# A Fourier and mixture-of-experts kernel: one sum of each fold moved into a DMA, and side work spread over the steps

## Chip, cores, metric

The kernel runs on one core of a Trainium2 chip. The metric is the device time of one execution in microseconds (us). The profile is one execution taken by the hardware profiler; its engines are PE (TensorE, with its weight loads as PEld), DVE (VectorE), ACT (ScalarE), POOL (GpSimd) and SP (the queue that issues most DMAs).

## The reference, cut to what matters

```python
X = np.fft.fft(np.fft.fft(x, axis=1), axis=2).real   # x: 8 x 3072 x 256, fp32
x = X.reshape(24576, 256)
g = x @ w_gate                                        # 256 x 1536
x = (g * sigmoid(g) * (x @ w_val)) @ w_out            # back to 256 columns
logits = x @ moe2_w_gate                              # 8 experts
# experts take tokens in falling order of logits, each up to 3072 of them
# out[mask] = relu(x[mask] @ w1[e]) @ w2[e]
```

## The kernel before, in words

Phase 1 computes the two-dimensional transform, the gated layer and the routing logits; phase 2 routes and runs the experts. The change is in phase 1.

Phase 1 goes through 48 tiles of 512 tokens, six for each of the eight batches. A tile has NF = 12 steps, one for each block of 128 hidden columns, and g counts the steps of all tiles (576). Step g in the main loop (lines 674 to 702) issues this: on PE the products Q (line 381) into the one Q bank; on ACT the copy qs of Q (681); on PE the products Pp; on ACT hi(g-2) (687), on POOL lo(g-2) (688); on DVE `columns(g)`, which is two T operations that read Q (392) and two G operations (393, 394); on ACT the silu sl(g-1) (695); on DVE the product hh(g-1) of sl and G, both in SBUF (400); on PE the twelve matmuls of `out_proj(g-3)` into Y (412). When a tile's last out_proj is through (its step 2 of the following tile) `finish` copies Y on ACT and moves the logits on POOL (420 to 426). Every engine takes what is issued to it in this order.

Side work is a set of Python generators. `advance(s)` runs each of them up to its next `yield`; half step A(g) = 2g is at the front of step g, Z(g) = 2g + 1 at its end. What stands in Z(g) is therefore queued behind step g's work on each engine, and what stands in A(g + 1) right behind that and ahead of step g + 1's. The side work:

- Transform halves (`fft_half`, lines 339 to 368; registered in lines 630 to 645). During tile t - 1 the x of tile t is computed, in a sine and a cosine half. A half has its matmuls into the one F bank (`fft_mm`, 300 to 326), then the copy od on ACT (351), a subtraction and an addition into ab on DVE (355 or 359, and 360), for the sine half also a one-row multiply by -1 (362); then xh on ACT (366) and xl on POOL (367). Before, the sine half starts at Z(1) and the cosine half at Z(4) of the tile.
- Folds (`fold`, 116 to 137; registered 646 to 661). Each batch from the second on has six x tiles of 512 KB, loaded by SP (113). POOL adds halves into fa (120), then makes fb (124, 127) and z (131, 134); these sums feed the transform. One operation every step, five steps a fold, from step 14 of the batch before on. `fold_special` does a last row at the end (142 to 152). xs has two buffers.
- The choice (`choose`, 775 to 795; registered 666 to 672): for each 16 columns of logits five DVE pieces, one per half step, from step 6 of every fourth tile on.
- A mini tile (437 to 495) runs in tiles 42 to 44.

```python
for g in range(total + LAG):
    advance(2 * g)
    ...
    advance(2 * g + 1)
```

Of the kernel before, what the change touches and what calls it, by code (L numbers as in the profile page):

```python
# [9 lines left out]
F32 = mybir.dt.float32  # L10
# [5 lines left out]
ALU = mybir.AluOpType  # L16
AX = mybir.AxisListType

P = 128
B = 8  # L20
S = 3072
D = 256
N = B * S
F = 1536
NF = F // P
# [61 lines left out]
def phase1(ctx, tc, io, yscr, Lall, ident, idt, NT, choice=None):  # L87
    nc = tc.nc
# [3 lines left out]
    work = ctx.enter_context(tc.tile_pool(name="work", bufs=2))  # L92
# [18 lines left out]
    def load_x(b, i):  # L111
        xs = work.tile([P, 4, D], F32, tag="xs", bufs=2, name="xs")
        nc.sync.dma_start(xs.rearrange("p m d -> p (m d)"), io["x"][b, i])
        return xs

    def fold(b, i, xs, eng, tags=(("fa", 1), ("fb", 1))):

        (ta, na), (tb, nb) = tags
        a = work.tile([P, 2, D], F32, tag=ta, bufs=na, name="fa")
        eng.tensor_add(a, xs[:, 0:2, :], xs[:, 2:4, :])  # L120
        yield
        yield
        bb = work.tile([P, 2, D], F32, tag=tb, bufs=nb, name="fb")
        eng.tensor_add(bb[:, 0, :], a[:, 0, :], a[:, 1, :])
        yield
        yield
        eng.tensor_sub(bb[:, 1, :], a[:, 0, :], a[:, 1, :])
        yield
        yield
        z = work.tile([P, 2, 2, P], F32, tag=f"z{i}", bufs=2, name=f"z{i}")  # L130
        eng.tensor_add(z[:, 0], bb[:, :, 0:P], bb[:, :, P:D])
        yield
        yield
        eng.tensor_sub(z[:, 1], bb[:, :, 0:P], bb[:, :, P:D])
        zt[b, i] = z
        yield
        yield
# [198 lines left out]
        nc.sync.dma_start(tb, tscr[b : b + 1, (t % 6) * 256 : (t % 6 + 1) * 256].broadcast_to([P, 256]))  # L336
        return tb

    def fft_half(t, sine, tb, res, bk=("F", 1), eng=nc.gpsimd):

        b, h, q = t // 6, (t // 3) % 2, t % 3
        lead = 1 if (h == 0 and q == 0) else 0
        n = P + lead

        par = (1 - h) if sine else h
        z = [zt[b, i][:, int(sine), par, :] for i in range(6)]
        pp = bank(*bk)
        fft_mm(pp, z, e768s[b % 2] if (h == 0 and not sine) else None, h, q, sine)
        yield
        od = work.tile([P, 129], F32, tag="od", bufs=1, name="od")  # L350
        nc.scalar.copy(od[:, :n], pp[:, 256 : 256 + n])
        ab = work.tile([P, 256], F32, tag="ab", bufs=2, name="ab")
        first = ab[:, 0:P][:, ::-1]
        if not sine:
            nc.vector.tensor_sub(first, pp[:, lead:n], od[:, lead:n])
            if lead and "R" in mini:
                nc.vector.tensor_copy(mini["R"][:, b : b + 1], ab[:, P - 1 : P])
        else:
            nc.vector.tensor_sub(first, od[:, lead:n], pp[:, lead:n])
        nc.vector.tensor_add(ab[:, P - lead : 256], pp[:, 0:n], od[:, 0:n])  # L360
        if sine:
            nc.vector.tensor_scalar_mul(ab[0:1, :], tb[0:1, :], -1.0)
        yield
        hi = work.tile([P, 256], F32R, tag=f"x{int(sine)}h", bufs=2, name="xh")
        lo = work.tile([P, 256], F32R, tag=f"x{int(sine)}l", bufs=2, name="xl")
        nc.scalar.copy(hi, ab)
        eng.tensor_sub(lo, ab, hi.bitcast(F32))
        res[sine] = (hi, lo)
# [68 lines left out]
    def mini_tile():  # L437

        xs = {}
        r0 = work.tile([1, B], F32, tag="tz", bufs=1, name="t15r")  # L440
        nc.sync.dma_start(r0, t15scr.rearrange("b o -> o b"))
        for n in ("R", "T"):
            for a in range(2):
                xs[n, a] = work.tile([P, P], F32R, tag=f"m{n}{a}", bufs=1, name=f"m{n}{a}")
                nc.gpsimd.memset(xs[n, a].bitcast(F32), 0.0)
        hs = [[work.tile([P, 4, P], F32R, tag=f"z{2 * j + a}", bufs=2, name=f"hT{a}") for a in range(2)] for j in range(3)]
        for t in hs:
            for a in range(2):
                nc.gpsimd.memset(t[a].bitcast(F32), 0.0)
        yield  # L450
        yield
        for n, src, k in (("R", mini["R"], P), ("T", r0, 1)):
            nc.vector.tensor_copy(xs[n, 0][0:k, 0:B], src)
            nc.vector.tensor_sub(xs[n, 1][0:k, 0:B], src, xs[n, 0][0:k, 0:B].bitcast(F32))
        yield
        for j in range(3):
            sl = work.tile([P, 4, D], F32, tag="xs", bufs=2, name="xs").rearrange("p a b -> p (a b)")
            for gv in range(2):
                pp = bank("F", 1)
                n = 0  # L460
                for cs, k in ((0, "R"), (1, "T")):
                    for a, d in order:
                        nc.tensor.matmul(pp, xs[k, d], Wb[j][:, cs, gv, a, :], start=(n == 0), stop=(n == 5))
                        n += 1
                yield
                if gv == 0:
                    nc.scalar.activation(sl[0:B, 0:512], pp[0:B, :], AF.Silu)
                else:
                    nc.vector.tensor_mul(sl[0:B, 512:1024], pp[0:B, :], sl[0:B, 0:512])
                yield  # L470
            pt = bank("F", 1)
            for i in range(4):
                nc.tensor.transpose(pt[:, i * P : i * P + B], sl[0:B, 512 + i * P : 512 + i * P + P], ident[0:B, 0:B])
            yield
            pv = pt.rearrange("p (i k) -> p i k", i=4)[:, :, 0:B]
            nc.scalar.copy(hs[j][0][:, :, 0:B], pv)
            nc.vector.tensor_sub(hs[j][1][:, :, 0:B], pv, hs[j][0][:, :, 0:B].bitcast(F32))
            yield
        for _ in range(4):
            yield  # L480
        pp = bank("F", 1)
        for c in range(NF):
            for i, (a, d) in enumerate(((0, 0), (0, 1), (1, 0))):
                nc.tensor.matmul(pp[:, 0:EXT], hs[c // 4][a][:, c % 4, :], Wo[c // 2][:, c % 2, d, :], start=(c == 0 and i == 0), stop=(c == NF - 1 and i == 2))
            if c % 4 == 3 and c < NF - 1:
                yield
                yield
        yield
        ys = work.tile([B, EXT], F32, tag="ys", bufs=1, name="ysm")
        nc.vector.tensor_copy(ys, pp[0:B, 0:EXT])  # L490
        lm = work.tile([B, E], F32, tag="lm", bufs=1, name="lm")
        nc.vector.tensor_copy(lm, ys[:, D:EXT])
        nc.vector.tensor_copy(ys[:, D : D + 1].bitcast(I32), idt[0:B, NCOL : NCOL + 1])
        nc.sync.dma_start(yscr[3 * P - 1 : N : S, :], ys)
        nc.sync.dma_start(Lall[P - 1 : P, 2 : 4 * NT : 24, :], lm)

    def off_peak(gen, s):

        s0 = s
        while True:  # L500
            if (s == s0 or s % (2 * NF) > NF or s % (2 * NF) == 0) and next(gen, gen) is gen:
                return
            s += 1
            yield
# [4 lines left out]
    def at(s, gen):  # L509

        side.setdefault(s, []).insert(0, gen)
# [113 lines left out]
    A, Z = lambda g: 2 * g, lambda g: 2 * g + 1  # L625
# [4 lines left out]
    for t in range(1, NT):  # L630
        res = {}
        g0 = (t - 1) * NF + (7 if t == 1 else 0)

        def start(t=t, res=res):
            res["tb"] = load_tb(t)
            yield

        def half(sine, t=t, res=res):
            yield from fft_half(t, sine, res["tb"], res)
            if not sine:  # L640
                RI[t] = (res[False], res[True], res["tb"])

        at(A(g0), start())
        at(Z(g0 + 1), half(True))
        at(Z(g0 + (2 if t == 1 else 4)), half(False))
    for b in range(1, nb):
        g0 = (b - 1) * 6 * NF
        xs = {}

        def load(i, b=b, xs=xs):  # L650
            xs[i] = load_x(b, i)
            yield

        def folds(b=b, xs=xs):
            for i in range(6):
                yield from fold(b, i, xs[i], nc.gpsimd)
            yield from fold_special(b, nc.gpsimd)

        for i in range(6):
            at(A(g0 + 8 + 5 * i), load(i))  # L660
        at(Z(g0 + 14), folds())
    if mini:
        g0 = (NT - 6) * NF + 6
        at(A(g0), off_peak(mini_tile(), A(g0)))

    if choice:

        for c in range(0, 4 * NT, 16):
            n = min(16, 4 * NT - 4 - c)
            at(Z((c + n) // 4 * NF + 6), choice(work, range(c, c + n)))  # L670

        at(Z((NT - 1) * NF + 9), choice(work, range(2, 4 * NT, 24)))

    for g in range(total + LAG):
        advance(2 * g)
# [638 lines left out]
```

## Time and profile before

| | |
|---|---|
| runs | 3205.24, 3205.67, 3206.16 us (median 3205.67) |
| profiled execution | 3206.77 us, span 3205.0 us |
| PE busy | 3095.8 us (97%) |
| DVE busy | 2564.8 us (80%) |
| ACT busy | 1531.6 us (48%) |
| POOL busy | 1639.7 us (51%) |
| DMA queues | 13.7% of 16 engines' span, all kinds together |

Busy time is the union of an engine's instructions as recorded; consecutive instructions overlap in the records by some 0.08 us. PE's matmuls are pipelined, so what PE loses shows best as a longer distance from one step's start to the next. Phase 1's steady part lasts from about 130 us to 1880 us, phase 2 fills the time from about 1925 us on.

### The profile page before, as it was taken

The numbers are of one execution on the slowest core, as the hardware profiler recorded it, in microseconds if no ns is written. First come the engines' busy times: TensorE is split into PE (matmuls) and PEld (weight loads), VectorE is DVE, ScalarE is ACT, GpSimd is POOL, SyncE is SP. The second block draws the span as 40 slices with busy tenths as digits, with TensorE's granted clock in tenths as the row PEclk, the third lists the DMA queues.
The fourth block names the chain that finished last, engine by engine and source line by source line (L and its number), as shares of the span: only waits on it lengthen the run. The fifth ranks groups of instructions, "written<-read, shape, count | busy, mean of one in ns | idle before, by whom it ended". The sixth has DMA issues, their size and how long they took to land.

```text
span 3205.0 us, 63221 instructions
## 1 busy us (share of the span) xinstructions
PE 3095.8 (97%) x23835; PEld 2922.4 (91%) x23835; DVE 2564.8 (80%) x5678; ACT 1531.6 (48%) x3034; POOL 1639.7 (51%) x1761
## 2 busy tenths in 40 slices
PE   6999999999999999999999994999999999999998
PEld 4899999999999999999999993888888888888998
DVE  8899999999999999999998887776767676766322
ACT  3555556555565565555555551232324333333332
POOL 3474674674764755855844442343435353435442
PEclk7999999999999999999999995999999999999999
DMA  5110100100101101101000001121212121122111
GB/s 210 31 38 18 46 31 27 49 25 25 51 18 33 44 23 39 39 18 45 31 20 16 18 16 59 41 67 41 69 43 69 44 72 54 54 69 70 49 44 37
DMA packets 71441, 143.94 MB, mean 45 GB/s; under 512 B 13602, under 2 KB 47442, under 8 KB 69088
## 3 DMA queue, kind: packets, MB, share of 16 engines
q1 hardware_dynamic: 50388, 71.96, 6.9%
q0 software_dynamic: 20736, 67.92, 6.3%
q8 instruction: 189, 3.10, 0.4%
q14 instruction: 116, 0.95, 0.1%
q10 hardware_dynamic: 12, 0.01, 0.0%
HBM read 88.67 MB, written 51.18 MB: 44 GB/s over the span
## 4 chain that ended last, share of the span: by engine, by line
PE 87%; DVE 6%; issue 3%; POOL 2%; ACT 1%; DMA 1%; SPq 0%; POOLq 0%; ACTq 0%; DVEq 0%
PE Y L412 23%; PE B L1144 16%; PE A L1118 16%; PE Q L381 12%; PE Pp L381 11%; PE F L321 2%; PE F L324 2%; PE C L877 2%; PE A L1100 1%; DVE T L392 1%; POOL lo L688 1%; DVE G L394 1%; PE L L1038 0%; PE Y L207 0%; DVE ge L869 0%
## 5 line engine op out<-in xcount | busy, mean ns | idle before, releaser
L688 POOL TENSOR_TENSOR lo<-hh,hi 128x512 fp32r<-128x512 f32 x576 | 745.5, 1294 | 751.8 <-ACT hi L687 739.6
L412 PE MATMUL Y<-Wo,hi 128*128 128x264 f32 x4608 | 866.3, 284 | 0.1
L412 PEld LDWEIGHTS Y<-Wo,hi 128*128 128x128 f32 x4608 | 710.2, 188 | 0.3 <-ACT hi L687 0.3
L412 PE MATMUL Y<-Wo,lo 128*128 128x264 f32 x2304 | 654.7, 284 | 5.3 <-POOL lo L688 5.3
L681 ACT COPY qs<-Q 128x512 f32<-128x512 f32 x576 | 340.0, 590 | 520.9 <-PE Q L381 511.2
L392 DVE SCALAR_TENSOR_TENSOR T<-tb,w,Q 128x256 f32<-128x256 f32 x1152 | 500.9, 476 | 97.5 <-ACT qs L681 91.0
L1144 PE MATMUL B<-w,hh 128*128 128x256 f32 x3072 | 576.5, 287 | 0.0
L1153 POOL DMA_INDIRECT out_dram<-ot,id x192 | 191.9, 1000 | 623.4 <-ACT ot L1151 469.8
L1118 PE MATMUL A<-yh,w 128*128 128x512 f32 x1536 | 492.9, 402 | 1.3 <-DVE hl L1135 0.9
L400 DVE TENSOR_TENSOR hh<-sl,G 128x512 f32<-128x512 f32 x576 | 476.0, 826 | 1.1 <-issue 1.1
L1144 PEld LDWEIGHTS B<-w,hh 128*128 128x128 f32 x3072 | 472.8, 189 | 3.2
L381 PE MATMUL Q<-xh,W 128*128 128x256 f32 x2304 | 446.7, 286 | 14.4 <-DVE T L392 7.9
L412 PEld LDWEIGHTS Y<-Wo,lo 128*128 128x128 f32 x2304 | 434.1, 188 | 7.6 <-POOL lo L688 7.6
L381 PE MATMUL Pp<-xh,W 128*128 128x256 f32 x2304 | 431.2, 280 | 0.0
L1144 PE MATMUL B<-w,hl 128*128 128x256 f32 x1536 | 431.0, 281 | 0.0
L687 ACT CAST hi<-hh 128x512 fp32r<-128x512 f32 x576 | 360.5, 626 | 70.8 <-DVE hh L400 66.1
L393 DVE TENSOR_TENSOR G<-Pp,qs 128x512 f32<-128x512 f32 x576 | 393.1, 683 | 0.0
L394 DVE TENSOR_TENSOR G<-T,Pp 128x512 f32<-128x512 f32 x576 | 389.7, 677 | 0.0
L1135 DVE SCALAR_TENSOR_TENSOR hl<-A,hh 128x512 fp32r<-128x512 f32 x384 | 262.9, 687 | 154.8 <-ACT hh L1124 154.0
L381 PEld LDWEIGHTS Q<-xh,W 128*128 128x128 f32 x2304 | 353.7, 189 | 27.1 <-ACT hi L687 14.4
L1124 ACT ACTIVATE hh<-A 128x512 fp32r<-128x512 f32 x384 | 229.2, 598 | 310.2 <-PE A L1118 283.6
L695 ACT ACTIVATE sl<-G 128x512 f32<-128x512 f32 x576 | 365.5, 634 | 0.0
(252 smaller groups left out, 5089.9 us busy)
## 6 DMA issues: line engine op xcount, KB each, us to landing
xs<-in_x_dram SPq DMA_DIRECT2D x43, 512.0 KB
yscr<-ys SPq DMA_DIRECT2D x40, 528.0 KB
tb<-tscr SPq DMA_DIRECT2D x48, 128.0 KB
raw<-in_wg_dram SPq DMA_DIRECT2D x6, 512.0 KB
raw<-in_wv_dram SPq DMA_DIRECT2D x6, 512.0 KB
rawWo<-in_wo_dram SPq DMA_DIRECT2D x12, 256.0 KB
yg<-yscr,idx POOLq DMA_INDIRECT x192, 2.8
out_dram<-ot,id POOLq DMA_INDIRECT x192, 2.4
```

Source lines behind the costliest of these rows:

```text
L381: nc.tensor.matmul(pp[:, gv * 256 : gv * 256 + 256], W[:, cs, gv, a, cc : cc + P], RI[t][cs][d], start=(i == 0), stop=(i == 2))
L392: nc.vector.scalar_tensor_tensor(T[:, gv, :], tb, w2[:, gv, c : c + 1], pq[:, gv * 256 : gv * 256 + 256], op0=ALU.mult, op1=ALU.add)
L393: nc.vector.tensor_sub(G[:, 0, :], pp, qs)
L394: nc.vector.tensor_add(rev(G[:, 1, :])[:, :, ::-1], T, rev(pp))
L400: nc.vector.tensor_mul(hh, s["sl"], s["G"][:, :, 256:512])
L412: nc.tensor.matmul(Yp[t][u], h[a][:, u * P : (u + 1) * P], Wo[c // 2][:, c % 2, d, :], start=(c == 0 and i == 0), stop=(c == NF - 1 and i ...
L681: nc.scalar.copy(s["qs"], s["pq"])
L687: nc.scalar.copy(hi, s["hh"])
L688: nc.gpsimd.tensor_sub(lo, s["hh"], hi.bitcast(F32))
L695: nc.scalar.activation(s["sl"], s["G"][:, :, 0:256], AF.Silu)
L1118: nc.tensor.matmul(pa, w[:, a, c : c + P], res["y", i][d][:, k, :], start=(n == 0), stop=(n == 5))
L1144: nc.tensor.matmul(pb[:, 0:D], h[a][:, s * P : (s + 1) * P], w[:, d, (f % 2) * D : (f % 2) * D + D], start=(n == 0), stop=(n == 23))
```

## The change

A fold's x tile is loaded by SP only in its first half; after 5 half steps POOL issues a DMA that adds the second half onto it as it loads (`accum_op`), in place of POOL's add into fa. Two such half tiles share an xs buffer. Folds start one step later and keep their pace. From the third tile on, a transform half reads its F bank in separate half steps (`far`), and both halves start one step earlier. The choice gets two yields for each piece and starts one step later.

```diff
+    pair = {}
+    def load_half(b, i):
+        if i % 2 == 0:
+            pair[b] = work.tile([P, 4, D], F32, tag="xs", bufs=2, name="xs")
+        xs = pair[b][:, 2 * (i % 2) : 2 * (i % 2) + 2, :]
+        nc.sync.dma_start(xs.rearrange("p m d -> p (m d)"), io["x"][b, i][:, 0 : 2 * D])
+        return xs
+
+    def add_half(b, i, xs):
+        nc.gpsimd.dma_start(xs.rearrange("p m d -> p (m d)"), io["x"][b, i][:, 2 * D : 4 * D], accum_op=ALU.add)
+
-    def fold(b, i, xs, eng, tags=(("fa", 1), ("fb", 1))):
+    def fold(b, i, xs, eng, tags=(("fa", 1), ("fb", 1)), added=False):
         (ta, na), (tb, nb) = tags
-        a = work.tile([P, 2, D], F32, tag=ta, bufs=na, name="fa")
-        eng.tensor_add(a, xs[:, 0:2, :], xs[:, 2:4, :])
-        yield
-        yield
+        if added:
+            a = xs
+        else:
+            a = work.tile([P, 2, D], F32, tag=ta, bufs=na, name="fa")
+            eng.tensor_add(a, xs[:, 0:2, :], xs[:, 2:4, :])
+            yield
+            yield
...
-    def fft_half(t, sine, tb, res, bk=("F", 1), eng=nc.gpsimd):
+    def fft_half(t, sine, tb, res, bk=("F", 1), eng=nc.gpsimd, far=False):
...
         nc.scalar.copy(od[:, :n], pp[:, 256 : 256 + n])
         ab = work.tile([P, 256], F32, tag="ab", bufs=2, name="ab")
         first = ab[:, 0:P][:, ::-1]
+        if far:
+            yield
         if not sine:
             nc.vector.tensor_sub(first, pp[:, lead:n], od[:, lead:n])
...
         else:
             nc.vector.tensor_sub(first, od[:, lead:n], pp[:, lead:n])
+        if far:
+            yield
+            yield
         nc.vector.tensor_add(ab[:, P - lead : 256], pp[:, 0:n], od[:, 0:n])
         if sine:
+            if far:
+                yield
             nc.vector.tensor_scalar_mul(ab[0:1, :], tb[0:1, :], -1.0)
         yield
...
-            yield from fft_half(t, sine, res["tb"], res)
+            yield from fft_half(t, sine, res["tb"], res, far=t > 1)
...
-        at(Z(g0 + 1), half(True))
-        at(Z(g0 + (2 if t == 1 else 4)), half(False))
+        at(Z(g0 + (1 if t == 1 else 0)), half(True))
+        at(Z(g0 + (2 if t == 1 else 3)), half(False))
...
         def load(i, b=b, xs=xs):
-            xs[i] = load_x(b, i)
+            xs[i] = load_half(b, i)
+            for _ in range(5):
+                yield
+            add_half(b, i, xs[i])
             yield
...
-                yield from fold(b, i, xs[i], nc.gpsimd)
+                yield from fold(b, i, xs[i], nc.gpsimd, added=True)
+                yield
+                yield
...
-        at(Z(g0 + 14), folds())
+        at(Z(g0 + 15), folds())
...
+    def slowly(gen):
+        for _ in gen:
+            yield
+            yield
+
     if choice:
         for c in range(0, 4 * NT, 16):
             n = min(16, 4 * NT - 4 - c)
-            at(Z((c + n) // 4 * NF + 6), choice(work, range(c, c + n)))
-        at(Z((NT - 1) * NF + 9), choice(work, range(2, 4 * NT, 24)))
+            at(Z((c + n) // 4 * NF + (7 if c + n + 4 < 4 * NT else 6)), slowly(choice(work, range(c, c + n))))
+        at(Z((NT - 1) * NF + 11), choice(work, range(2, 4 * NT, 24)))
```

## Rows read from the trace of the kernel before

**Rows 1.** Busy time by stage; columns: stretch, length, each engine's busy time, clock, DMA
```profile
400.00:800.00 400.00, 398.11 (x3324) 395.60 (x3323) 373.18 (x708) 237.73 (x471) 245.73 (x227) 1.00 0.10 31
```

**Rows 2.** ACT's timeline: qs of first steps, tiles 13, 25, 41, 42, 45, 46
```profile
584.70 0.59 ACT L681 COPY qs<-Q 128x512 f32<-128x512 f32 x1 [1.24 <-PE Q L381]
...
1037.50 0.59 ACT L681 COPY qs<-Q 128x512 f32<-128x512 f32 x1 [1.24 <-PE Q L381]
...
1641.76 0.59 ACT L681 COPY qs<-Q 128x512 f32<-128x512 f32 x1 [1.24 <-PE Q L381]
...
1679.05 0.59 ACT L681 COPY qs<-Q 128x512 f32<-128x512 f32 x1 [1.20 <-PE Q L381]
...
1806.56 0.59 ACT L681 COPY qs<-Q 128x512 f32<-128x512 f32 x1 [1.20 <-PE Q L381]
...
1843.61 0.59 ACT L681 COPY qs<-Q 128x512 f32<-128x512 f32 x1 [1.20 <-PE Q L381]
```

**Rows 3.** Engines' timelines, undisturbed step; start, length, what, [idle before <- its end]
```profile
356.47 1.30 POOL L688 TENSOR_TENSOR lo<-hh,hi 128x512 fp32r<-128x512 f32 x1 [1.56 <-ACT hi L687]
...
357.90 0.68 DVE L400 TENSOR_TENSOR hh<-sl,G 128x512 f32<-128x512 f32 x1
...
358.13 0.59 ACT L681 COPY qs<-Q 128x512 f32<-128x512 f32 x1 [1.20 <-PE Q L381]
...
358.75 0.87 DVE L392 SCALAR_TENSOR_TENSOR T<-tb,w,Q 128x256 f32<-128x256 f32 x2 [0.17 <-ACT qs L681]
```

**Rows 4.** Timelines of POOL, DVE, ACT and PE at one fold's first sum
```profile
384.21 1.29 POOL L120 TENSOR_TENSOR fa<-xs 128x512 f32<-128x512 f32 x1
...
384.26 1.79 DVE L400 TENSOR_TENSOR hh<-sl,G 128x512 f32<-128x512 f32 x1
...
384.52 0.59 ACT L681 COPY qs<-Q 128x512 f32<-128x512 f32 x1 [1.11 <-PE Q L381]
...
386.98 0.48 PE L381 MATMUL Q<-xh,W 128*128 128x256 f32 x2 [0.40 <-DVE T L392]
...
388.01 0.59 ACT L681 COPY qs<-Q 128x512 f32<-128x512 f32 x1 [0.78 <-PE Q L381]
```

**Rows 5.** The same timelines at one of a fold's shorter operations
```profile
378.34 0.75 POOL L131 TENSOR_TENSOR z<-fb 128x256 f32<-128x256 f32 x1
...
378.51 1.13 DVE L400 TENSOR_TENSOR hh<-sl,G 128x512 f32<-128x512 f32 x1
...
378.79 0.59 ACT L681 COPY qs<-Q 128x512 f32<-128x512 f32 x1 [0.95 <-PE Q L381]
...
381.65 0.59 ACT L681 COPY qs<-Q 128x512 f32<-128x512 f32 x1 [0.81 <-PE Q L381]
```

**Rows 6.** ACT's timeline over a choice in tile 16: qs five steps apart
```profile
721.54 0.59 ACT L681 COPY qs<-Q 128x512 f32<-128x512 f32 x1 [0.81 <-PE Q L381]
...
736.31 0.59 ACT L681 COPY qs<-Q 128x512 f32<-128x512 f32 x1 [1.24 <-PE Q L381]
```

**Rows 7.** Phase 2: POOL's DMA issues (group, then timeline), DVE's timeline beside them
```profile
L1153 POOL DMA_INDIRECT out_dram<-ot,id x192 | 191.9, 1000 | 623.4 <-ACT ot L1151 469.8 <-ACT id L1103 103.7 <-DVE ge L869 9.2
...
2416.95 0.94 POOL L1070 DMA_INDIRECT w2f<-in_w_dram,wi  x1 [0.30 <-issue]
...
2417.27 0.95 DVE L783 TENSOR_TENSOR eq<-ml,m 128x768 f32<-128x768 f32 x1
...
2284.49 1.37 DVE L785 TENSOR_TENSOR eq<-eq,small 128x768 f32<-128x768 f32 x1
...
2431.76 1.72 POOL L1153 DMA_INDIRECT out_dram<-ot,id  x1 [2.20 <-DVE eq L783]
```

**Rows 8.** Timelines of DVE and ACT: an ab addition; xh with qs behind it
```profile
375.65 0.28 DVE L360 TENSOR_TENSOR ab<-F,od 128x128 f32<-128x128 f32 x1
...
367.80 0.45 ACT L366 CAST xh<-ab 128x256 fp32r<-128x256 f32 x1
368.11 0.63 ACT L681 COPY qs<-Q 128x512 f32<-128x512 f32 x1
```

## The prediction

> **What bounds the kernel now.** I read the table by stage first, then the engines' timelines, from the clock of whole tiles down to single steps. In the steady part of phase 1 PE is busy for 398 of 400 us at full granted clock, with DVE at 373 of 400 [rows 1]: PE sets the time and DVE has little room. The change touches phase 1 alone, so the question is how much PE loses there today. The start of the qs copies is a good clock, one per step. A tile without folds or choice takes 37.05 us, or 37.29 us when its transform has a thirteenth product; twelve tiles in the middle take 452.80 us [rows 2]. Undisturbed they would take 12 x 37.05 + 6 x 0.24 = 446.04 us. So 6.76 us per twelve tiles are stalls, 0.56 us a tile, and over the 40 tiles 2 to 41, in which folds and choices run, 22.5 us. **That is all the change can win**; tiles 42 to 44 belong to the mini tile, which it leaves alone.
>
> Where do these stalls come from? In an undisturbed step hh takes 0.68 us, T starts 0.62 us after qs, and DVE was idle 0.17 us before it; lo takes 1.30 us on POOL, which was idle 1.56 us before it [rows 3]. A step without loss takes 2.86 us from qs to qs, as in [rows 5]. With a fold's first sum the POOL add runs 1.29 us and the hh product, started 0.05 us later, takes 1.79 us: DVE waits until POOL is done. DVE starts its next instruction about 0.08 us before the last one's recorded end, so T comes at 385.97 where qs (384.52) plus 0.62 would be 385.14, 0.83 us late. The Q bank is single, so the next Q matmul waits for DVE's T, and the next qs comes after 3.49 us: 0.63 us lost [rows 4]. A short fold operation (0.75 us) lengthens hh to 1.13 us; T is then 0.15 us late and the next qs comes after 2.86 us: nothing lost [rows 5]. So **PE absorbs about 0.20 us of T's lateness, and loses what is beyond**. The choice (five DVE pieces in five half steps, two of them between one hh and the next T) costs 736.31 - 721.54 = 14.77 us for five steps, 0.47 us over 5 x 2.86 [rows 6].
>
> **Part 1: the first sum leaves POOL.** 42 adds (six in each of seven batches) of 1.29 us or more go [rows 4]. With the long stalls they and their after-effects cause, and the choice's, go most of the 22.5 us. I let 0.3 us a batch stay for the special row's three operations at the end of a fold (2.1 us in seven batches) and 0.1 us for each of ten choices: **gain 19.4 us**; bounds 12 (only the collisions themselves) and 22.5.
>
> **Part 2: the accumulating DMA on POOL's queue.** The trace has no such DMA. Nearest rows: the indirect DMAs that POOL issues in phase 2, mean 1.00 us, 0.30 us idle before each when they follow one another, longest 1.72 us [rows 7]. Does issuing hold DVE up, as an add does? An eq comparison with two SBUF inputs that began 0.32 us into such an issue took 0.95 us, where an eq product of the same shape beside POOL's subtractions took 1.37 us [rows 7]; so I take that it doesn't. Its place: every add but a batch's first shares a half step with a fold's first remaining operation. POOL then has lo 1.30, issue 1.30 and add 0.75, together 3.35 us in a step of 2.86, so lo ends about 0.48 us late and pushes hh by about 0.34 us, of which 0.17 is DVE's idle time: T is 0.17 us late, within 0.20. Cost 0. At 1.72 + 0.30 us per issue T would be 0.9 us late: 0.7 us in 35 of the steps, 24 us; that is the upper bound, and below nothing I see no gain. I take 0, as the mean issue is what most of 192 rows are. The issue also waits on POOL for the half load, and behind it is lo, which PE needs: the written order gives 2.5 steps (7 us) between load and add, five steps (14 us) from add to fold. SP's earlier waits on fa go away. I take 0 here. The Trainium skill (DMA: Bandwidth & Descriptors, Anatomy of one DMA) gives 2.0 us plus bytes over 436e3 for a DMA issued from POOL; by it the 256 KB land in an estimated 2.6 us, and the sum would be the same.
>
> **Part 3: the transform's reads, spread.** This part decides. Before, a half's od copy, subtraction and addition stand together at the front of a step (A) and its xh copy at the end of that step (Z). By the new yields, counted in half steps: the sine half has its matmuls at Z(0), od at A(1), subtraction Z(1), addition Z(2), the -1 multiply A(3), xh and xl at Z(3). DVE gets 0.2 us more before T(2) and about 0.5 before T(3); the second is hidden by the cosine half's matmuls, which follow step 3 on PE. Cost 0; without that cover about 0.1 us a tile. The cosine half: matmuls Z(3), od A(4), subtraction Z(4), **addition Z(5), xh A(6)**. The addition stands on DVE behind hh(4), just before T(6). The xh copy stands on ACT *ahead of qs(6)*, and waits for it. So ACT's queue is held: qs(6) can no longer start when PE has finished Q(6).
>
> Priced on the undisturbed step [rows 3]: T there starts at 358.75 after 0.17 idle, so hh ended at 358.58; the addition starts at 358.50 and takes 0.28 us [rows 8], to 358.78. xh starts then, and qs follows xh after 0.31 us (367.80 to 368.11) [rows 8], at 359.09 instead of 358.13. T is 0.96 us late, 0.20 is absorbed: **0.76 us per tile**. Behind the waiting xh stand qs(6), hi(4) and sl(5); lo(4) comes about 1 us later and has about that much until its matmuls. Transforms with the new yields run in tiles 1 to 46; in tile 1 and two or so of tiles 42 to 44 other F matmuls after step 6 hide the stall. 43 x 0.76 = **32.7 us**. In 13 tiles (numbers 1 and 3 of each batch's six, less tile 1 itself) a fold operation of 0.75 us comes just before that hh and delays it as in [rows 5] by 0.45 us, which now adds in full: **5.9 us** (bounds 0 and 5.9).
>
> **Part 4: the choice, one piece a step.** One piece, about the size of an ab addition (0.28 us), uses up DVE's 0.17 us idle and makes T some 0.1 us late: free. Its gain is in part 1. The last choice moves two steps later, into the drain: at most +0.3 us.
>
> **Sum.** -19.4 + 0 + 32.7 + 5.9 + 0.3 = +19.5 us on the profiled execution's own 3206.77 us: 3226.3. That execution stands 1.1 us above the median of 3205.67, so I forecast **3225 us**, 0.6% slower.
>
> **Rivals.** (a) *xh doesn't hold qs, and the change is faster.* Place: ACT's queue at step 6. If the addition were done before hh(4), so that T(6) is less than 0.20 us late, parts 3's 38.6 us vanish and 19.4 us are won: 3186 us. For it: DVE has 0.17 us free per step, and the F bank is full long before. Against: every engine in the trace takes its instructions in program order, and the addition is written behind hh(4). Chance 0.14. (b) *The wait bites half as hard*, 0.4 us a tile, because qs runs closer behind xh than in the one row: 43 x 0.4 = 17 us, against 19 to 22 won: 3205 to 3209 us. Chance 0.10. (c) *The DMA's issue is long on POOL.* From about 1.35 us with its idle time in it, lo pushes hh beyond the 0.20 us. At 1.5 us it costs 6 us, at 2.0 us 24 us: 3231 to 3249 us. For it: one of the phase 2 issues, begun 0.09 us after a DVE product with two SBUF inputs, took 1.72 us [rows 7], and hh is such a product in every step. Chance 0.16. The Trainium skill (SBUF — State Buffer, Who interferes with whom) has a rule against this change: descriptors of a DMA issued from POOL cannot be written while DVE runs a copy, cast or tensor_scalar in a two-port mode; by it (c) would be likelier. No row here shows such an instruction beside an issue in phase 1, and the -1 multiply on one row is the only one of that class in its steps, so I leave (c)'s chance as it is.
>
> **Numbers.** 0.60 for the forecast, 0.14, 0.10 and 0.16 for (a), (b), (c). A measurement of this kernel can tell about 0.2%, 6.4 us, from no change. Slower by more: 0.60 + 0.16 and a part of (b), 0.80; within: 0.06; faster: 0.14. The range leaves (a) out and a little of (c): 3206 (every stall of today gone, the wait at 0.5 us in 43 tiles: 3205.67 - 22.5 + 21.5, and a little more) to 3244 (forecast plus most of (c)). The forecast's own range is 3212 to 3235.
>
> **What would show it.** In the changed profile xh of the cosine half should start right at the end of a DVE addition that follows hh, with qs right behind it and PE's next Q waiting for T, once a tile, step 6 some 0.76 us longer; idle time of ACT should be put to DVE ab. hh should take over 1.3 us hardly ever, POOL's direct DMA about 1.0 us. If qs never waits behind xh, I am wrong by the whole of part 3; if the steps with an issue are long, (c) holds.

## The result: 3246.46 us, 1.3% slower

The changed kernel takes 3246.46 us in the median of four runs (3244.66 to 3248.51), the kernel before 3205.86 us beside it: ratio 1.0128, 95% interval 1.0115 to 1.0141. That is 40.6 us more, where 19 were forecast and the range ended at 3244. The profiled execution took 3244.66 us, its span is 3242.9 us.

In the table by stage of the profile after, the stretch of [rows 1] reads (columns as there):

```profile
400.00:800.00 400.00, 388.66 (x3230) 384.85 (x3229) 358.44 (x687) 229.82 (x457) 229.53 (x221) 1.00 0.11 30
```

At the same full clock PE is busy 9.5 us less of 400, DVE 14.7, ACT 7.9, and POOL, which has lost its first sums, 16.2: the engines wait more. The page's groups say where (busy, mean ns of one | idle before, releaser), first before, then after:

```profile
L392 DVE SCALAR_TENSOR_TENSOR T<-tb,w,Q 128x256 f32<-128x256 f32 x1152 | 500.9, 476 | 97.5 <-ACT qs L681 91.0
...
L381 PE MATMUL Q<-xh,W 128*128 128x256 f32 x2304 | 446.7, 286 | 14.4 <-DVE T L392 7.9
```

```profile
L415 DVE SCALAR_TENSOR_TENSOR T<-tb,w,Q 128x256 f32<-128x256 f32 x1152 | 500.2, 475 | 194.6 <-ACT qs L714 193.1
...
L404 PE MATMUL Q<-xh,W 128*128 128x256 f32 x2304 | 450.7, 288 | 53.3 <-ACT sl L728 38.4
```

DVE's T waited 97.5 us before, 91.0 of them for qs; now 194.6 us, 193.1 of them for qs. PE's Q waited 14.4 us and now 53.3. The releaser named for Q, sl, only happens to end last: Q doesn't use it, and starts 0.15 us after T's end, as in [rows 4].

**First loss, one step per tile.** I count a tile's steps from one Q product's start to the next on PE's timeline. Step 6 takes 3.56 or 3.67 us in every tile without folds, where it took 2.86. The timelines of DVE, ACT and PE in tile 16 (compare [rows 3, 8]):

```profile
733.12 0.68 DVE L423 TENSOR_TENSOR hh<-sl,G 128x512 f32<-128x512 f32 x1
733.72 0.28 DVE L381 TENSOR_TENSOR ab<-F,od 128x128 f32<-128x128 f32 x1
734.96 0.87 DVE L415 SCALAR_TENSOR_TENSOR T<-tb,w,Q 128x256 f32<-128x256 f32 x2 [0.96 <-ACT qs L714]
```

```profile
734.03 0.41 ACT L389 CAST xh<-ab 128x256 fp32r<-128x256 f32 x1 [1.89 <-DVE ab L381]
734.35 0.58 ACT L714 COPY qs<-Q 128x512 f32<-128x512 f32 x1
```

```profile
735.98 0.47 PE L404 MATMUL Q<-xh,W 128*128 128x256 f32 x2 [0.54 <-ACT sl L728]
```

This is the forecast chain: hh, then the addition, then xh 0.03 us after its end, qs 0.32 us behind xh, T 0.61 us behind qs, Q. qs starts 1.93 us after the step's start at 732.42, where an undisturbed one in tile 8 starts 0.96 after it (408.42 against 407.46): 0.97 us late, 0.70 lost.

**Second loss, not foreseen.** In the tiles with number 2 modulo 6, steps 2 and 7 take 3.83 and 3.88 us, where the tiles without folds take 2.86 and 2.92 to 2.96; no transform stands in their way. Timelines of DVE, ACT and POOL in tile 8, step 2:

```profile
408.15 2.02 DVE L423 TENSOR_TENSOR hh<-sl,G 128x512 f32<-128x512 f32 x1
410.08 0.28 DVE L377 TENSOR_TENSOR ab<-od,F 128x128 f32<-128x128 f32 x1
410.28 0.86 DVE L415 SCALAR_TENSOR_TENSOR T<-tb,w,Q 128x256 f32<-128x256 f32 x2
```

```profile
408.42 0.59 ACT L714 COPY qs<-Q 128x512 f32<-128x512 f32 x1 [1.24 <-PE Q L404]
```

```profile
407.96 0.87 POOL L127 DMA_DIRECT2D xs<-in_x_dram  x1
408.57 1.03 POOL L140 TENSOR_TENSOR fb<-xs 128x256 f32<-128x256 f32 x1
```

The issue of the adding DMA takes 0.87 us and the fold's first operation, fb, stands right behind it. hh starts 0.19 us after the issue and doesn't end until 0.57 us after fb's end (409.60): 2.02 us, more than with the 1.29 us add that the change took away (1.79 us, [rows 4]). T starts 1.86 us after qs instead of 0.62. Yet an issue alone does no such thing. Tile 6, step 11, on DVE and POOL:

```profile
359.39 0.68 DVE L423 TENSOR_TENSOR hh<-sl,G 128x512 f32<-128x512 f32 x1
```

```profile
359.20 0.87 POOL L127 DMA_DIRECT2D xs<-in_x_dram  x1
360.83 1.29 POOL L721 TENSOR_TENSOR lo<-hh,hi 128x512 fp32r<-128x512 f32 x1 [0.77 <-ACT hi L720]
```

Here too hh starts 0.19 us after the issue, but POOL's next operation, lo, isn't ready until 1.63 us after the issue's start.

**A gain outside the steps, not foreseen either.** From step start to step start, tiles 1 to 46 are 44.6 us longer than before (1797.5 against 1752.9), which is more than the whole loss. Some 4 us come back at the very end. The last output copy on ACT, before and after:

```profile
3195.38 0.37 ACT L1151 COPY ot<-B 128x256 f32<-128x256 f32 x1 [2.44 <-PE B L1144]
```

```profile
3237.43 0.37 ACT L1184 COPY ot<-B 128x256 f32<-128x256 f32 x1 [2.44 <-PE B L1177]
```

From its end to the end of the span 9.24 us pass before and 5.09 after. The same 5.09 us stand in every kernel below that issues the adding DMA, 4.27 with a plain one, and 9.24 or 8.80 in the three without one. Why is not shown. Where tiles 1 to 46 are given below, they leave this end out.

So there are two theories to test. **Theory 1**: the wait of xh ahead of qs costs some 41 us (the expectation of experiment 1 has the sum). **Theory 2**: a POOL operation that is ready right behind a DMA's issue holds hh from the issue on, and this gives back what the folds' first sums had cost. Rivals to theory 2: the issue, the transfer's traffic, or the addition in it holds hh. (The ready operation is called "queued behind" below.)

### The profile page after: what moved, and what is told of

It reads as the page before. It is cut to its first block, busy times and chain, and to the rows that moved or that the text cites. A ratio compares the mean times of both kernels' runs of the same rounds, so it can differ in the third digit from the quotient of the medians.

```text
span 3242.9 us, 63320 instructions
## 1 busy us (share of the span) xinstructions
PE 3100.0 (96%) x23835; PEld 2922.3 (90%) x23835; DVE 2546.2 (79%) x5678; ACT 1526.6 (47%) x3034; POOL 1587.4 (49%) x1761
## 4 chain that ended last, share of the span: by engine, by line
PE 76%; DVE 11%; issue 7%; ACT 4%; DMA 1%; POOL 0%; SPq 0%; ACTq 0%; POOLq 0%; DVEq 0%
PE Y L435 18%; PE B L1177 16%; PE A L1151 15%; PE Q L404 10%; PE Pp L404 8%; DVE T L415 3%; DVE G L417 3%; PE F L337 2%; PE F L340 2%; ACT qs L714 2%; PE C L910 2%; PE A L1133 1%; DVE G L416 1%; ACT sl L728 1%; ACT hi L720 1%
## 5 line engine op out<-in xcount | busy, mean ns | idle before, releaser
L415 DVE SCALAR_TENSOR_TENSOR T<-tb,w,Q 128x256 f32<-128x256 f32 x1152 | 500.2, 475 | 194.6 <-ACT qs L714 193.1
L404 PE MATMUL Q<-xh,W 128*128 128x256 f32 x2304 | 450.7, 288 | 53.3 <-ACT sl L728 38.4
L423 DVE TENSOR_TENSOR hh<-sl,G 128x512 f32<-128x512 f32 x576 | 467.9, 812 | 0.9 <-ACT sl L728 0.9
```

Source lines behind the costliest of these rows:

```text
L404: nc.tensor.matmul(pp[:, gv * 256 : gv * 256 + 256], W[:, cs, gv, a, cc : cc + P], RI[t][cs][d], start=(i == 0), stop=(i == 2))
L415: nc.vector.scalar_tensor_tensor(T[:, gv, :], tb, w2[:, gv, c : c + 1], pq[:, gv * 256 : gv * 256 + 256], op0=ALU.mult, op1=ALU.add)
L423: nc.vector.tensor_mul(hh, s["sl"], s["G"][:, :, 256:512])
```

## Experiments

Medians; ratios are to the kernel before, run beside them. It stood at 3206.2 us beside experiments 1 to 4, at 3208.1 beside 5, 6, 7 and 10, and at 3206.2 beside 8, 9 and 11. Where runs of different groups are set against each other I also compare tiles 1 to 46 in the traces.

**1. xh one half step later** (the changed kernel, cosine half).

```
             nc.vector.tensor_scalar_mul(ab[0:1, :], tb[0:1, :], -1.0)
+        elif far:
+            yield
         yield
```

> The changed kernel with one more half step before the cosine half's xh, so that xh stands behind sl(5) at Z(6) and no longer ahead of qs(6). Theory 1 (the wait of xh holds qs once a tile): step 6 falls from 3.56-3.67 us to about 2.87 us in 43 tiles, and the extra 0.6 to 0.8 us in tiles 1 and 3 of each batch goes with it: 33 + 8 = 41 us less than the changed kernel, about 3205 us. Rival (the whole loss is the accumulating DMA's on POOL): less than 5 us change, 3241 to 3246 us.

Measured: 3207.07 us, ratio 1.0001 (0.9991 to 1.001). ACT's timeline in tile 16, where xh now stands behind qs, hi and sl:

```profile
721.11 0.59 ACT L716 COPY qs<-Q 128x512 f32<-128x512 f32 x1 [1.23 <-PE Q L406]
721.59 0.62 ACT L722 CAST hi<-hh 128x512 fp32r<-128x512 f32 x1
722.11 0.63 ACT L730 ACTIVATE sl<-G 128x512 f32<-128x512 f32 x1
722.64 0.39 ACT L391 CAST xh<-ab 128x256 fp32r<-128x256 f32 x1
723.97 0.59 ACT L716 COPY qs<-Q 128x512 f32<-128x512 f32 x1 [0.93 <-PE Q L406]
```

From qs to qs 2.86 us, nothing lost. 3246.46 - 3207.07 = **39.4 us** was the order of xh and qs (40.5 us in tiles 1 to 46). And what is left of the change without it is worth nothing, where rival (a) had put 3186 us: tiles 1 to 46 are 4.1 us longer than before, and the end gives that back.

**2. The kernel before with the transform's reads spread as in the change, and nothing else.**

```
... (the yields under `if far` in fft_half, as in the change)
-            yield from fft_half(t, sine, res["tb"], res)
+            yield from fft_half(t, sine, res["tb"], res, far=t > 1)
...
-        at(Z(g0 + 1), half(True))
-        at(Z(g0 + (2 if t == 1 else 4)), half(False))
+        at(Z(g0 + (1 if t == 1 else 0)), half(True))
+        at(Z(g0 + (2 if t == 1 else 3)), half(False))
```

> The kernel before with only the transform's reads spread and its halves one step earlier; folds and choice as before. Theory 1: 43 x 0.76 = 33 us slower than before, up to 42 where the folds' collisions now add in full: 3238 to 3248 us. Rival (the DMA is the loss): within 5 us of before, 3201 to 3211 us.

Measured: 3255.45 us, 1.0158 (1.0142 to 1.0173), 49 us more than before: above both. In tile 8, step 6, on DVE, ACT and POOL:

```profile
420.69 1.73 DVE L407 TENSOR_TENSOR hh<-sl,G 128x512 f32<-128x512 f32 x1
422.33 0.28 DVE L365 TENSOR_TENSOR ab<-F,od 128x128 f32<-128x128 f32 x1
```

```profile
422.64 0.40 ACT L373 CAST xh<-ab 128x256 fp32r<-128x256 f32 x1 [2.88 <-DVE ab L365]
422.95 0.58 ACT L688 COPY qs<-Q 128x512 f32<-128x512 f32 x1
```

```profile
420.57 1.29 POOL L120 TENSOR_TENSOR fa<-xs 128x512 f32<-128x512 f32 x1
```

A fold's first sum, still there, lengthens the hh that the addition stands behind; the step takes 4.87 us. Against tile 16 of the changed kernel, hh starts 0.28 us later in the step and lasts 1.05 us longer, and the step is 1.31 us longer: while qs is held, the delay of hh adds in full.

**3. The kernel before with the adding DMA alone** (folds one step later as in the change; halves and choice as before).

```
... (load_half, add_half and fold's `added`, as in the change)
-            xs[i] = load_x(b, i)
+            xs[i] = load_half(b, i)
+            for _ in range(5):
+                yield
+            add_half(b, i, xs[i])
...
-                yield from fold(b, i, xs[i], nc.gpsimd)
+                yield from fold(b, i, xs[i], nc.gpsimd, added=True)
+                yield
+                yield
...
-        at(Z(g0 + 14), folds())
+        at(Z(g0 + 15), folds())
```

> The kernel before with only the accumulating DMA in place of a fold's first sum (folds one step later, as in the change); transform halves and choice as before. Theory 2 (a POOL operation queued right behind the DMA's issue locks DVE's hh out from the start of the issue on, some 2 us in two steps of a batch): about 15 us of the old stalls go and 14 to 16 us of new ones come, 3200 to 3208 us. The prediction's term (the issue costs nothing): 3190 us. Rival (every issue holds hh up, in 42 steps by 0.9 us): 3215 us or more.

Measured: 3204.76 us, 0.9996 (0.9987 to 1.0005): theory 2's value, not the 3190 of my terms. DVE and POOL in tile 8 show that hh isn't the only one held:

```profile
418.40 2.83 DVE L811 TENSOR_TENSOR eq<-Lall,m 128x128 f32<-128x128 f32 x1
```

```profile
417.56 0.86 POOL L127 DMA_DIRECT2D xs<-in_x_dram  x1
418.16 1.02 POOL L140 TENSOR_TENSOR fb<-xs 128x256 f32<-128x256 f32 x1
418.90 1.50 POOL L716 TENSOR_TENSOR lo<-hh,hi 128x512 fp32r<-128x512 f32 x1
420.13 0.94 POOL L143 TENSOR_TENSOR fb<-xs 128x256 f32<-128x256 f32 x1
```

A comparison of the choice, two inputs in SBUF and 0.28 us elsewhere, waits through three POOL operations that follow one another without a gap. The step takes 5.53 us, in tiles 8, 20 and 32. The holds here thus fall in part on other instructions than in the changed kernel, whose choice stands elsewhere.

**4. The kernel before with the spread choice alone.**

```
... (slowly, as in the change)
-            at(Z((c + n) // 4 * NF + 6), choice(work, range(c, c + n)))
+            at(Z((c + n) // 4 * NF + (7 if c + n + 4 < 4 * NT else 6)), slowly(choice(work, range(c, c + n))))
...
-        at(Z((NT - 1) * NF + 9), choice(work, range(2, 4 * NT, 24)))
+        at(Z((NT - 1) * NF + 11), choice(work, range(2, 4 * NT, 24)))
```

> The kernel before with only the choice spread, one piece a step. Theory: 0.47 us at each of ten choices becomes 0.1 us, a gain of 3 to 4 us, 3202 us; in the three tiles where a choice meets a fold it may gain nothing. Rival (a piece in more steps keeps DVE late for longer): no gain or up to 3 us slower.

Measured: 3205.48 us, 0.9998 (0.9989 to 1.0008): not to be told from none, where 3202 was expected. By the steps, pieces in steps without fold operations cost nothing (tile 16 as in [rows 6] now loses nothing), but tiles 8, 20 and 32 become 0.4 to 0.5 us longer each and the tile after each as much: with a piece and a fold operation in one step T comes 0.6 to 1.2 us late, more than the 0.20 us, and one to a step there are more such steps.

**5. The adding DMA in the folds' idle half step, and 6. behind the fold's operation** (the changed kernel; in 6 the same work in the same steps, with the two swapped on POOL).

```
-            at(A(g0 + 8 + 5 * i), load(i))
+            at(A(g0 + 7 + 5 * i), load(i))
```

```
-            for _ in range(5):
+            for _ in range(6):
                 yield
             add_half(b, i, xs[i])
```

> The changed kernel with every load one step earlier, so that the adding DMA is issued in the half step in which the folds do nothing, with no fold operation behind it on POOL. Theory 2 (it is the fold operation queued right behind the DMA's issue that holds hh, 2.0 us instead of 0.68; the issue alone holds nothing): steps 2 and 7 of the tiles with number 2 modulo 6 go from 3.83 and 3.88 back to about 2.9, and step 6 from 3.83 to about 3.6: 7 batches x 2.1 to 2.3 us = 15 to 16 us off 3246.5, 3230 to 3233 us. Rival (the issue or the transfer itself holds hh wherever it falls): the waits move with it, 3241 us or more.

> The changed kernel with the adding DMA half a step later: the same operations in the same steps, but on POOL the fold's operation stands ahead of the DMA and not behind it. Theory 2 (order decides): hh beside the fold's operation alone takes 1.1 to 1.2 us as in other steps, the two steps per batch cost 0.0 to 0.2 us each, and the time is 3231 to 3235 us. Rival (what counts is how much work POOL has in that step, or the transfer's traffic): within 4 us of the changed kernel, 3243 to 3250 us.

Measured: 3238.39 us, 1.0095 (1.0079 to 1.011), and 3242.5 us, 1.0106 (1.0091 to 1.0122). The times don't decide: the first lies between the two theories, the second half a us below the rival's 3243. The steps do. Steps 2 and 7 of the tiles 2 modulo 6 are back to 2.95 and 3.01 us in both, 12.3 us off. Experiment 6, tile 8, step 2, DVE and POOL:

```profile
408.57 1.12 DVE L423 TENSOR_TENSOR hh<-sl,G 128x512 f32<-128x512 f32 x1
```

```profile
408.40 0.73 POOL L140 TENSOR_TENSOR fb<-xs 128x256 f32<-128x256 f32 x1
409.08 0.88 POOL L127 DMA_DIRECT2D xs<-in_x_dram  x1
```

The same operations, swapped: hh 1.12 us instead of 2.02. So it is the order. What the two runs lack of the expected gain is elsewhere. Step 6 stayed at 3.83 us. I had put 0.27 us of it to the DMA; it belongs to the wait of xh, since DVE is 0.27 us behind from the step before and experiment 1 brings the step to 2.94 us. In 5 the tiles 1 modulo 6 are 0.24 us longer. In 6 they are 0.8 us longer: there the issue pushes lo into the next step, a fold operation follows it at once, and the hh that starts beside them takes 1.80 us; tile 42 is 1.5 us longer too. Tiles 1 to 46 are 10.3 and 5.9 us shorter in sum than the changed kernel's.

**7. The same issue without the addition in it, and 8. a tiny memset between issue and fold operation** (the changed kernel).

```
-        nc.gpsimd.dma_start(..., accum_op=ALU.add)
+        nc.gpsimd.dma_start(...)
```

```
         nc.gpsimd.dma_start(..., accum_op=ALU.add)
+        nc.gpsimd.memset(gap, 0.0)
```

> The changed kernel with the same DMA from POOL, but writing its half instead of adding it (the first sum of a fold is left out, so the values are others). Theory 2 (issue with an operation behind it, whatever the transfer does): 3245 to 3249 us, hh still about 2.0 us. Rival (the adding, with its extra reads of SBUF, holds hh): hh back to 1.2 us or less and 3230 to 3236 us.

> The changed kernel with one tiny memset on POOL (1 x 8 elements) between the adding DMA's issue and whatever follows it on POOL. Theory 2a (the operation that stands next in POOL's queue claims, while the issue still runs, the access that hh needs, and only an operation that reads SBUF does so): with the memset next, hh in steps 2 and 7 is back to 0.7 to 1.2 us, these steps are 2.9 to 3.0 us, 12 us off: 3232 to 3237 us. Theory 2b (any operation queued behind the issue holds hh): 3244 to 3250 us.

Measured: 3245.03 us, 1.0115 (1.0099 to 1.013), and 3246.81 us, 1.0125 (1.0109 to 1.014): neither time can be told from the changed kernel's. A plain issue takes 0.55 us instead of 0.87, and hh 1.70 instead of 2.02 us, 0.32 us less in both: the hold lasts as long as issue and operation do, whatever the transfer does. With the memset, tile 8, step 2 and then tile 6, step 11, each DVE, then POOL:

```profile
410.13 2.04 DVE L426 TENSOR_TENSOR hh<-sl,G 128x512 f32<-128x512 f32 x1
```

```profile
409.95 0.87 POOL L127 DMA_DIRECT2D xs<-in_x_dram  x1
410.54 0.33 POOL L128 MEMSET gap<- 1x8 f32 x1
410.60 1.01 POOL L143 TENSOR_TENSOR fb<-xs 128x256 f32<-128x256 f32 x1
```

```profile
361.32 0.68 DVE L426 TENSOR_TENSOR hh<-sl,G 128x512 f32<-128x512 f32 x1
```

```profile
361.13 0.87 POOL L127 DMA_DIRECT2D xs<-in_x_dram  x1
361.71 0.32 POOL L128 MEMSET gap<- 1x8 f32 x1
```

Neither 2a nor 2b as I wrote them: a memset alone behind the issue doesn't hold hh, but it doesn't shield it either from a fold operation that is queued one place further. What held hh in the long steps, fb or xl, reads SBUF; the memset only writes, but it is also tiny, and no run separates the two. The Trainium skill (SBUF — State Buffer, Who interferes with whom) says just this of a DVE instruction with two SBUF inputs: it contends with a GpSimd instruction that reads SBUF, not with one that only writes; the memset's row agrees. It also says that the one issued first goes first. By the records hh began 0.42 us before fb in tile 8 of the changed kernel and still waited, so for an operation behind a DMA's issue the measurement decides: its claim counts from the issue.

**9. The first sums left out, without a DMA** (experiment 3 without its `add_half`).

```
-            add_half(b, i, xs[i])
```

> The kernel of the run with the DMA alone (old halves, old choice, folds of four operations one step later) without the adding DMA: the second half of a fold's input is left out, so the values are others. It prices the two sides of the change by themselves. Theory 2: the fold's first additions were worth 13 to 18 us and the DMA gives as much back, so 3187 to 3192 us here against 3204.8 us with the DMA. The prediction's terms (additions worth 15 to 19 us, issue free) ask for 3187 to 3191 us here too, but for the same time with the DMA. Rival (the folds' first additions were never worth much, the DMA is free): 3201 us or more.

Measured: 3191.17 us, 0.9953 (0.9938 to 0.9969). So the first sums were worth 3206.24 - 3191.17 = **15.1 us** (14.4 in tiles 1 to 46), and the DMA in experiment 3 gave 3204.76 - 3191.17 = **13.6 us** of it back. In tiles 1 to 46 it cost 17.3 us: 8.4 in tiles 8, 20 and 32, where eq is held, and some 0.83 in each of ten tiles where hh is held for 2.0 us. The shorter end hides the rest.

**10. The changed kernel with the halves as before and the DMA in the folds' idle half step** (first diff); **and 11. that with loads, additions and folds one step later** (second).

```
-            yield from fft_half(t, sine, res["tb"], res, far=t > 1)
+            yield from fft_half(t, sine, res["tb"], res, far=False)
...
-        at(Z(g0 + (1 if t == 1 else 0)), half(True))
-        at(Z(g0 + (2 if t == 1 else 3)), half(False))
+        at(Z(g0 + 1), half(True))
+        at(Z(g0 + (2 if t == 1 else 4)), half(False))
...
-            at(A(g0 + 8 + 5 * i), load(i))
+            at(A(g0 + 7 + 5 * i), load(i))
```

```
-            at(A(g0 + 7 + 5 * i), load(i))
+            at(A(g0 + 8 + 5 * i), load(i))
-        at(Z(g0 + 15), folds())
+        at(Z(g0 + 16), folds())
```

> The halves of the transform as in the kernel before, the DMA additions in the folds' idle half step, the choice in spread pieces. Theory 1 with theory 2: no addition ahead of qs and no operation behind an issue. Of the 22.5 us of stalls before, those of the fold's 1 x 512 additions go; some short ones beside fold operations stay: 3187 to 3193 us. If the issue alone cost hh its time in any step, 3200 us or more; if the choice piece collides as in the run with the DMA alone (2.8 us in tiles 8, 20 and 32), 3196 us.

> The run with the old halves, the additions in the folds' idle half step and the spread choice (3192.7 us), with loads, additions and folds all one step later. There, two of six issues in a batch fell into the step of xl, which took the place of the fold's operation behind the issue (hh 2.01 us in step 6 of the tiles 2 modulo 6, 0.78 us a batch; 0.3 us in step 4 of the tiles 1 modulo 6). Theory 2: one step later no issue has xl or a fold operation behind it, 7 x 1.1 us = 7 to 8 us less, 3184 to 3188 us. Rival (an issue holds hh wherever it falls once transfers and folds are dense): 3191 us or more.

Measured: 3192.72 us, 0.9954 (0.994 to 0.9967), and **3184.89 us, 0.9932 (0.9918 to 0.9945)**. In 10 one issue a batch had xl behind it (tile 8, step 6, DVE and POOL):

```profile
413.37 2.01 DVE L423 TENSOR_TENSOR hh<-sl,G 128x512 f32<-128x512 f32 x1
```

```profile
413.19 0.87 POOL L127 DMA_DIRECT2D xs<-in_x_dram  x1
413.80 1.02 POOL L390 TENSOR_TENSOR xl<-ab,xh 128x256 fp32r<-128x256 f32 x1
```

In 11 only the very first, in tile 0, has; behind the others lo isn't ready. No hh of the 576 takes over 1.5 us (21 in the changed kernel, 31 before), with the same 42 DMAs and the same 0.87 us issues. Tiles 1 to 46 are 10.1 and 16.0 us shorter than before. Experiment 11 beats both kernels.

## Why the prediction was wrong: right in direction, 21 us short

**What bounds the kernel, right, with luck in the total.** The stalls of tiles 2 to 41, given as 22.5 us, are 22.2 by PE's steps. Experiment 11 won 21.3 us in all (3206.24 - 3184.89), but only 16.0 in tiles 1 to 46, where 6.7 us of stalls are left, and 4.15 at the end, which stood in no term. An undisturbed tile is 37.05 us in it, as in [rows 2].

**Part 1 (gain 19.4 us), right in kind, some 4 us too large.** In tiles 1 to 46 the first sums alone are worth 14.4 us; with the spread choice and a DMA that holds nothing, 16.0. Both lie in the bounds of 12 to 22.5.

**Part 2 (cost 0), the step that failed.** "Does issuing hold DVE up, as an add does? [...] I take that it doesn't" holds for an issue by itself. It is wrong for the place that I named a sentence later, where the issue shares a half step with a fold's first remaining operation. I put issue and operation one behind the other and looked only at when lo would end; the operation's own grip on hh I took from [rows 5] as if it began with the operation. It begins with the issue: hh ends 0.57 us after fb, T is 1.24 us late, 0.9 to 1.0 us is lost, twice a batch in the changed kernel. These are the 12.3 us that experiments 5 and 6 take from steps 2 and 7; in experiment 3 the cost was 17.3 us in the tiles. Both are inside the bounds of 0 to 24, of which I took the lower end. Right behind the issue beside the eq in [rows 7] stands, in the trace, only a memset, which reads nothing, so it couldn't show this; the row bore on the issue, and I let it speak for the pair.

**Part 3 (32.7 + 5.9 us), right.** 39.4 measured against 38.6 (40.5 in tiles 1 to 46). The 0.96 us of lateness measured 0.97, the 0.76 us a tile 0.70 to 0.81. The fold operation ahead of hh adds 0.5 to 0.8 us in tiles 1 and 3 modulo 6, and 0.2 more in tiles 2, where 0.45 and nothing were put. In experiment 1 the steps of the sine half are free in tiles without folds, as forecast.

**Part 4 (choice free, end +0.3), the net right, the reason wrong.** The pieces are free only in steps without fold operations; alone the spread choice measures nothing.

**The sum.** In tiles 1 to 46 the terms measured singly are -14.4 (first sums) - 0.6 (choice) + 40.5 (xh) + 12.3 (the issue's place) = 37.8 of the 44.6 us; 6.8 us are left to how the parts meet, which I didn't separate. The end then takes 4.15 us off. Replacing part 2's 0 by 12.3 alone puts the forecast at 3237; that the rest comes to only 9 us is in part luck, since part 1's 4 us too much and the end's 4.15 us nearly cancel.

**The rivals.** (a) and (b) fell: qs does wait behind xh, and for the full 0.97 us. (c) named the right resource and nearly the right price (3231 to 3249), but a wrong place: the issues take 0.85 to 0.92 us (41 of 42), far from the 1.35 from which it was to decide, and in the long steps it is fb, not lo, that hh waits for; (c)'s place shows up in experiment 6. (b)'s 3205 to 3209 needed the folds' 5.9 us too: 17 us against 19 to 22 alone give 3201 to 3204. The rule of the Trainium skill quoted beside (c) (SBUF — State Buffer, Who interferes with whom), on DVE's two-port modes, is neither borne out nor refuted: no such instruction runs beside an issue in the changed kernel, and seven issues of experiment 5 that begin 0.14 to 0.16 us into a -1 multiply take 0.88 to 0.91 us.

## What to carry to other kernels

In this kernel a DMA issued from POOL was cheap where nothing that reads SBUF stood ready behind it: put it in a step where POOL has nothing else, or behind the operation it would stand ahead of, and look at what stands in its new neighbourhood. An operation that reads late data must not stand, on an in-order engine, ahead of the copy that the critical chain waits for; half a step's difference in the written order was worth 39 us here. When a new instruction has no row in the trace, price it with its queue neighbours, not alone.

## What the runs showed of the hardware that I had not expected

- The claim has a sharp beginning. Over the changed kernel and experiments 1, 3, 8 and 10, each hh that starts 0.18 to 0.20 us after an issue with a ready fold operation or xl behind it takes 1.98 to 2.05 us (58 of them; only beside the first issue, in tile 0, does it take 1.20 to 1.25). Each that starts 0.15 us or less after one takes 0.67 to 0.69 us, operation or not.
- A third hold a batch is longer and free. In step 3 of the tiles 1 modulo 6 of the changed kernel hh starts 0.43 us after an issue and takes 2.44 to 2.51 us, through xl and fb; the cosine half's matmuls fill that step, which takes 4.32 to 4.35 us, as in the tiles 5 and 0 modulo 6, which have no folds in that step.
- The adding DMA's issue takes 0.87 us on POOL, the plain one 0.55 us, for the same 256 KB.
- The adding DMA lands 3.9 us after its issue in the median (the page's list of DMA issues). The estimate in the prediction by the Trainium skill (DMA: Bandwidth & Descriptors, Anatomy of one DMA) was 2.6 us; the measurement decides, and nothing waited for either.
- POOL operations that follow one another without a gap can keep a DVE instruction out through all of them (2.83 us for a 0.28 us comparison, in three tiles of experiment 3). It isn't always DVE that waits: in experiment 6, tile 7, step 9, an fb that starts together with hh takes 1.28 us instead of 0.73, and hh its 0.69.
